# Gates stored as twelve lines, weight measurements two steps later, final scatters of half rows without an order between them, and the eighth block asked for first

## The chip, the cores and the metric

The kernel runs on one core of a Trainium2 chip. The metric is the device time of one execution in microseconds (us). Three runs of the kernel before gave 1245.0, 1250.6 and 1256.08 us, so the median is 1250.6.

## The reference

A block-local attention feeds two mixture-of-experts layers. The attention (2 batches, 8 heads, 768 positions, head size 64) gives `x` with 1536 rows (tokens) of 512. The first layer routes every token to one of 8 experts, the second mixes all 8:

```python
logits = x @ w_gate                      # first layer, N = 1536, E = 8, F = 1024
expert_idx = np.argmax(logits, axis=1)
probs = softmax(logits); gate_w = probs[np.arange(N), expert_idx]
for e in range(E):
    out[mask_e] = gate_w[mask_e, None] * (np.maximum(x[mask_e] @ w1[e], 0) @ w2[e])

P = np.exp(x @ w_gate - max)             # second layer
for _ in range(8):
    P /= P.sum(1, keepdims=True) + 1e-09
    P /= P.sum(0, keepdims=True) + 1e-09
    P *= N / E
for e in range(E):
    out += P[:, e:e+1] * (np.maximum(x @ w1[e], 0) @ w2[e])
```

## The kernel before

The engines are TensorE (PE), VectorE (DVE), ScalarE (ACT), GpSimd (POOL) and SyncE (SP, which only starts DMAs here). Each runs its own instructions in order. Up to the end of the first layer a scheduler of the language sets the order in which each engine gets them; the second layer is written out by hand on a clock of ticks.

**Routing.** While the attention ends, `rows_out` transposes each tile of 128 tokens, copies it out of PSUM on ACT (line 533, three buffers `xn`) and stores it to `xd` in HBM (line 534, SP's queue). `experts`, `ranks` and `by_lane` work out on DVE which expert each token has and which row of which block it takes. `row_i` (line 653) holds the result, and `seat_i` (line 672) the rows to which results go. After the last routing matmul, `warm` (line 174) issues 100 small matmuls on PE, whose results nothing reads.

**First layer.** Tokens are sorted into blocks of 256 rows with one expert each. There are at least `NMIN` = 6 and at most 13; with these inputs there are seven. For each block POOL gathers two tiles of 128 rows (line 1034, `xb<-xd,row_i`; it waits for all stores to `xd`), PE transposes them (1066), ACT and DVE split them into a high part (`xh`, 1071) and a low part (`xl`, 1072), and `layer1` (979) and `layer2` (1001) multiply by weights that are split in the same way (`wh` on ACT at 944, `wl` on DVE at 946). The weights go through a ring of four 512 KB buffers `kx`. The gather of the first block is followed on POOL by a memset of `wgq` (1043).

While block n is computed, `compute` calls `step()` 18 times; the even calls take the next step of loading and splitting weights (`ahead`), the odd ones one list of `more`. `more` holds the gate work and eight pieces of second-layer weights, each as a row of steps (`plain`), a new piece every four steps:

```python
return [lambda: p.load(raw), idle, idle, lambda: p.measure(junk), p.measured, p.rate, ...]
each = -(-len(more) // (NMIN - 1))
```

`measure` (740, ACT) sums the squares of a piece and needs its load to have landed. `gate_square` (1138, ACT) sums the squares of the second gate's weights into `wgq`. `gates` (1155 to 1162: seven operations on DVE, one on ACT) works out each token's gate weight, and `gates_out` (1165) stores it to `gd` with one DMA from a tile of 128 partitions by 12 columns, so that neighbours in a column lie 4 bytes apart in HBM. As far as their operands allow, the scheduler puts these steps earlier than they are written. `gd` is read much later, by the gathers at line 850.

After the sixth block all engines load the number of blocks (1180) and branch:

```python
with tc.If(count > NMIN) as beyond:      # 1208
    rest(NMIN, cur)                      # starts with tc.If(count > n + 1), 1201
with beyond.Else():
    ...                                  # exactly six blocks
```

`rest` fetches and computes further blocks, and its own `Else` runs the last block (`final`). With seven blocks an engine falls through the first branch and jumps at the second.

**Second layer.** `first` (1365) and `second` (1451) compute each expert's products in seven block products of half-size matrices. The tail of the last expert adds the results into `acc` on DVE (1482) and scatters finished rows to `out` from POOL (1486). For the last pair of tiles the products come in the order i = 0, 1, 3, 2, 5, 4, 6: i = 5 completes the upper half of the second tile's rows, i = 4 the first tile, i = 6 the lower half of the second tile. Scatters are at i = 4 and i = 6, whole rows each. All write to the tensor `out`, so each waits for the one before.

## Time and profile before

| what | us |
|---|---|
| median of three runs | 1250.6 |
| the profiled execution | 1249.01 |
| its span, first to last instruction | 1247.2 |
| PE busy in the span | 1181.1 |
| DVE busy | 972.6 |
| ACT busy | 846.0 |
| POOL busy | 265.9 |

All times in the text are microseconds from the start of the span. A row of a timeline gives the start, the duration, the engine, the line, the operation with its operands, how many of them were merged, and in square brackets how long the engine had been idle before it and what it waited for. A wait with several causes is put down to the last one. `PEclk` is the clock that TensorE was granted, as a share of full speed.

### The profile page before, as it was taken

Reading aid. Unit: us, or ns where it says so; the run is one execution under the profiler, and the core shown is the slowest. Engines: PE = TensorE matmul, PEld = TensorE weight load, DVE = VectorE, ACT = ScalarE, POOL = GpSimd, SP = SyncE. Lnnn points to the kernel's source line nnn. Section 1 sums busy time; section 2 is a strip of 40 time slices with the busy share of each in tenths; the row PEclk is TensorE's granted clock in tenths of the full one; section 3 lists DMA queues with packets and bytes.
Section 4 is the critical chain, followed back from the end, with each engine's and each line's share of the span. In section 5 each row is a group of like instructions: output and inputs, shape, how many; then the busy total and the mean of one; then the engine's idle time right before and its main releaser. Section 6 shows DMA issues by size and latency. Waiting matters only on the chain. (4 is left out here: it accounts for less than half of the span.)

```text
span 1247.2 us, 27484 instructions
## 1 busy us (share of the span) xinstructions
PE 1181.1 (95%) x10473; PEld 1044.1 (84%) x10473; DVE 972.6 (78%) x1950; ACT 846.0 (68%) x1595; POOL 265.9 (21%) x331
## 2 busy tenths in 40 slices
PE   6898799999889999999999999999999999999997
PEld 5776688888778788888888888888888888888886
DVE  6695578884588898897878788788978878796763
ACT  5585467774677767776877677677767767776440
POOL 4351212312221220120121112111211211121011
PEclk9899799999999999999999999999999999999999
DMA  9947687862335543665556566555656655663201
GB/s 206 205 97 206 155 275 257 253 208 96 112 111 157 140 130 96 161 148 142 131 119 141 145 162 146 144 115 122 156 137 161 138 135 126 138 149 94 68 35 52
DMA packets 186496, 179.79 MB, mean 144 GB/s; under 512 B 35872, under 2 KB 159520, under 8 KB 185968
## 3 DMA queue, kind: packets, MB, share of 16 engines
q1 hardware_dynamic: 159648, 136.41, 38.6%
q0 software_dynamic: 26704, 41.50, 17.9%
q8 instruction: 85, 1.39, 0.5%
q14 instruction: 59, 0.48, 0.1%
HBM read 131.38 MB, written 15.53 MB: 118 GB/s over the span
## 5 line engine op out<-in xcount | busy, mean ns | idle before, releaser
L1365 PEld LDWEIGHTS <-w1h 128*128 128x128 f16 x2688 | 258.3, 98 | 46.0 <-issue 15.9
L1451 PEld LDWEIGHTS <-hh 128*128 128x128 f16 x2688 | 263.4, 98 | 32.0 <-issue 1.2
L1365 PE MATMUL fx<-kx,w1h 128*128 128x256 f16 x1472 | 257.3, 272 | 8.2 <-ACT c L1372 4.6
L1451 PE MATMUL gx<-w2l,hh 128*128 128x256 f16 x768 | 209.3, 273 | 1.1 <-DVE w2l L780 1.1
L1451 PE MATMUL gx<-w2h,hh 128*128 128x256 f16 x768 | 209.3, 273 | 1.0 <-DVE acc L1482 1.0
L1451 PE MATMUL gx<-w2h,hl 128*128 128x256 f16 x768 | 209.3, 273 | 0.0
L1365 PE MATMUL fx<-kx,w1l 128*128 128x256 f16 x736 | 200.5, 272 | 0.0
L1365 PE MATMUL fa<-kx,w1h 128*128 128x256 f16 x1104 | 193.7, 273 | 0.7 <-ACT yb L1113 0.7
L1372 ACT ACTIVATE c<-fx,kap 128x256 f32<-128x256 f32 x288 | 134.5, 473 | 79.3 <-PE fx L1365 78.8
L1451 PE MATMUL ga<-w2h,hh 128*128 128x256 f16 x576 | 157.6, 274 | 0.0
L1451 PE MATMUL ga<-w2l,hh 128*128 128x256 f16 x576 | 157.6, 274 | 0.0
L1451 PE MATMUL ga<-w2h,hl 128*128 128x256 f16 x576 | 157.5, 273 | 0.0
L1365 PE MATMUL fa<-kx,w1l 128*128 128x256 f16 x552 | 150.7, 273 | 0.0
L1365 PEld LDWEIGHTS <-w1l 128*128 128x128 f16 x1344 | 131.4, 98 | 17.2 <-issue 1.8
L1451 PEld LDWEIGHTS <-hl 128*128 128x128 f16 x1344 | 131.7, 98 | 16.7 <-issue 1.3
L1420 DVE TENSOR_TENSOR hl<-c,hh 128x1024 f16<-128x1024 f32 x96 | 117.1, 1220 | 26.4 <-ACT hh L1417 25.7
L1417 ACT CAST hh<-c 128x1024 f16<-128x1024 f32 x96 | 99.8, 1040 | 34.6 <-DVE c L1414 34.2
L1493 ACT ACTIVATE y<-gx,pws 128x256 f32<-128x256 f32 x144 | 68.2, 474 | 79.9 <-PE gx L1451 62.2
L753 POOL DMA_DIRECT2D raw<-raw x77 | 77.1, 1031 | 210.3 <-DVE w2l L780 97.4
L1375 DVE SCALAR_TENSOR_TENSOR c<-fa,kap,c 128x512 f32<-128x512 f32 x96 | 71.7, 747 | 46.3 <-PE fa L1365 39.9
L1408 DVE SCALAR_TENSOR_TENSOR hl<-c,hh 128x768 f16<-128x768 f32 x96 | 91.2, 950 | 15.4 <-ACT hh L1405 15.4
L1484 POOL DMA_DIRECT2D acc<-y x36 | 31.4, 871 | 336.8 <-ACT c L1372 265.9
(263 smaller groups left out, 2438.6 us busy)
## 6 DMA issues: line engine op xcount, KB each, us to landing
raw<-in_moe_w SPq DMA_DIRECT2D x228, 128.0 KB, 3.5
kx<-in_moe_w SPq DMA_DIRECT2D x56, 512.0 KB, 5.0
kx<-xohd SPq DMA_DIRECT2D x147, 128.0 KB, 3.3
kx<-xold SPq DMA_DIRECT2D x147, 128.0 KB, 3.1
acc<-y POOLq DMA_DIRECT2D x72, 256.0 KB, 4.5
raw<-raw POOLq DMA_DIRECT2D x77, 128.0 KB, 3.6
raw<-in_moe_w SPq DMA_DIRECT2D x38, 256.0 KB, 3.6
vt<-in_v SPq DMA_DIRECT2D x16, 240.0 KB, 7.5
```

The source lines that it names most:

```text
L753: nc.gpsimd.dma_start(out=self.raw[:, to], in_=self.raw[:, of], accum_op=ALU.add)
L1365: nc.tensor.matmul(p, l[:, a, kc * P : (kc + 1) * P], r[:, j, kc], start=new and kc == 0 and m == 0, stop=kc == K2 - 1 and m == 2, skip_gr ...
L1372: nc.scalar.activation(c[:, q], p, f, scale=k_)
L1375: nc.vector.scalar_tensor_tensor(out=c[:, q], in0=x, scalar=k_, in1=c[:, q], op0=ALU.mult, op1=ALU.add)
L1408: nc.vector.scalar_tensor_tensor(out=h[1][:, :3], in0=raw, scalar=0.0, in1=h[0][:, :3], op0=ALU.max, op1=ALU.subtract)
L1417: nc.scalar.copy(h[0][:, 3:], c)
L1420: nc.vector.tensor_tensor(out=h[1][:, 3:], in0=c, in1=h[0][:, 3:], op=ALU.subtract)
L1451: nc.tensor.matmul(p, l, r, start=new and f == 0 and m == 0, stop=f == F2 - 1 and m == 2, skip_group_check=True)
L1484: nc.gpsimd.dma_start(out=to, in_=gs[0], accum_op=ALU.add)
L1493: nc.scalar.activation(gs[h][:, d], p, AF.Copy, scale=w)
```

## The change

1. `gate_square` may not be issued before the latest `layer1` result on ACT; `gates` not before the latest on DVE. `gates` begins at step 3 of `more` in place of 2.
2. `gates_out` first transposes the 128 by 12 gates on PE, copies them to `gt` (12 partitions of 128) on ACT, and stores 12 lines of 512 bytes.
3. In `plain` two more idle steps stand between a piece's load and its measurement; all that follows moves by two. `more` grows from 39 to 41 lists, `each` from 8 to 9 a block.
4. The branch after the sixth block asks first for an eighth block (`rare`), then for a seventh, which is now straight code. PE gets a hint that the first branch is taken.
5. At the end the second tile of each pair is scattered in two halves of 256 columns, at i = 5 and i = 6, through `half_i` (two small DVE operations at tick 118). All final scatters are declared independent of each other.

```diff
         def gate_square():
             sq = wq.tile([P, KC * E], F32, name="wgsq")
-            nc.scalar.activation(sq, wg2_sb, AF.Square, accum_out=wgq)
+            with tc.issue_after(taken[-1][0].ins):
+                nc.scalar.activation(sq, wg2_sb, AF.Square, accum_out=wgq)
...
-            return [lambda: p.load(raw), idle, idle, lambda: p.measure(junk), p.measured, p.rate, lambda: (p.raw_hi(), p.sums(fast=True)), lambda: (p.raw_lo(), p.sum4(fast=True)),
+            return [lambda: p.load(raw), idle, idle, idle, idle, lambda: p.measure(junk), p.measured, p.rate, lambda: (p.raw_hi(), p.sums(fast=True)), lambda: (p.raw_lo(), p.sum4(fast=True)),
...
         def gates():
             sh = [P, NTB, E]
-            nc.vector.tensor_tensor(out=gex, in0=lg, in1=mx.unsqueeze(2).to_broadcast(sh), op=ALU.subtract)
+            with tc.issue_after(taken[-1][1].ins):
+                nc.vector.tensor_tensor(out=gex, in0=lg, in1=mx.unsqueeze(2).to_broadcast(sh), op=ALU.subtract)
...
         def gates_out():
-            nc.sync.dma_start(out=gd.rearrange("(t p) o -> p (t o)", p=P), in_=gate)
+            pt = ps_m.tile([NTB, P], F32, tag="m", name="pt")
+            nc.tensor.transpose(pt, gate, ident)
+            nc.scalar.copy(gt, pt)
+            nc.sync.dma_start(out=gd.rearrange("(t p) o -> t (p o)", p=P), in_=gt)
...
-            [(0, [gate_square, gate_rate]), (2, [gates, lambda: None, gates_out])]
+            [(0, [gate_square, gate_rate]), (3, [gates, lambda: None, gates_out])]
...
+        def hint():
+            tc.mark_branch_hint_location("rare", hint="LikelyTaken", engines=[mybir.EngineType.PE])
...
+                if n == NMIN - 1:
+                    own_ += [[]] * (HINT + 1 - len(own_))
+                    own_[HINT] = own_[HINT] + [hint]
...
-        with tc.If(count > NMIN) as beyond:
-            rest(NMIN, cur)
+        with tc.If(count > NMIN + 1, label="rare") as beyond:
+            nxt, steps = fetch(NMIN + 1)
+            compute(NMIN, cur, steps, nxt)
+            rest(NMIN + 1, nxt)
         with beyond.Else():
-            for fs in early():
-                for f in fs:
-                    f()
+            with tc.If(count > NMIN) as odd:
+                final(NMIN, cur)
+            with odd.Else():
+                for fs in early():
+                    for f in fs:
+                        f()
...
-            if e == E - 1 and i in (4, 6):
-                nc.gpsimd.indirect_dma_start(
-                    out=out, out_offset=bass.IndirectOffsetOnAxis(ap=token_i[:, t : t + 1], axis=0), in_=acc[:, t], in_offset=None,
-                    bounds_check=NT - 1, oob_is_err=True,
+            if e == E - 1 and i in (4, 5, 6):
+                if i == 4:
+                    to, at_, rows, n = out, token_i[:, t : t + 1], acc[:, t], NT
+                else:
+                    to, at_ = out.rearrange("t (h d) -> (t h) d", h=2), half_i[:, t - HTB, 6 - i : 7 - i]
+                    rows, n = acc[:, t, d], 2 * NT
+                put = nc.gpsimd.indirect_dma_start(
+                    out=to, out_offset=bass.IndirectOffsetOnAxis(ap=at_, axis=0), in_=rows, in_offset=None,
+                    bounds_check=n - 1, oob_is_err=True,
                 )
+                tc.declare_no_dep(put.ins, group="rows", reason="disjoint rows")
+                tc.add_to_no_dep_group("rows", put.ins)
```

How the change moves instructions, at three places. The line numbers in the rows of the change are its own, two to thirty above those of before.

**Routing, SP and ACT.** SP's queue at the end of the attention, before: the last loads of weights for the second layer (`raw`), the stores of rows (`xd<-xn`), the store of the gates (`gd<-gate`), then loads of block numbers.

```order
L167 DMA raw_93<-in_moe_w 128x256
L534 DMA xd<-xn 128x512 x3
L1165 DMA gd<-gate 128x12x1
L534 DMA xd<-xn 128x512 x3
L1045 TENSOR_LOAD eblk_i
L1045 ISA x2
```

The same place in the change:

```order
L169 DMA raw_94<-in_moe_w 128x256
L167 DMA raw_95<-in_moe_w 128x2x256
L168 DMA raw_95<-in_moe_w 128x256
L169 DMA raw_95<-in_moe_w 128x256
L536 DMA xd<-xn 128x512 x6
L1047 TENSOR_LOAD eblk_i
L1047 ISA x2
L1128 TENSOR_LOAD eblk_i
```

The store of the gates no longer stands among the stores of rows; it comes late in the second block, between loads of first-layer weights (`L1172 DMA gd<-gt 12x128`). ACT at the same place, before: copies of rows, the exponential of the gates (`gex`), measurements of three pieces (`raw,ssq`), the gate's squares (`wgsq,wgq`), the branch for the first expert (`eblk_i`), then the first weight split:

```order
L533 COPY xn<-pr 128x512 x2
L1156 ACTIVATE gex<-gex 128x96
L533 COPY xn<-pr 128x512 x4
L740 ACTIVATE raw_91,ssq_1730<-raw_91 128x1024
L1138 ACTIVATE wgsq,wgq<-wg_sb 128x32
L740 ACTIVATE raw_92,ssq_1730<-raw_92 128x1024
L740 ACTIVATE raw_93,ssq_1730<-raw_93 128x1024
L1126 TENSOR_LOAD eblk_i
L1127 COMPARE_AND_BRANCH
L1127 UNCONDITIONAL_BRANCH x2
L944 CAST wh_1763<-kx 128x1024
```

In the change:

```order
L535 COPY xn<-pr 128x512 x6
L742 ACTIVATE raw_93,ssq_1732<-raw_93 128x1024
L742 ACTIVATE raw_94,ssq_1732<-raw_94 128x1024
L742 ACTIVATE raw_95,ssq_1732<-raw_95 128x1024
L1128 TENSOR_LOAD eblk_i
L1129 COMPARE_AND_BRANCH
L1129 UNCONDITIONAL_BRANCH x2
L946 CAST wh_1765<-kx 128x1024
```

The exponential and the squares are gone from this place; the squares stand behind the first block's `layer1`, the exponential inside the second block.

**The branch, PE.** Before, after the sixth block's last product (`py`): the load of the block count, two branches, and the seventh block's first products (`ph`):

```order
L1001 MATMUL py_3499<-wh_1767,hl 128x512
L1180 TENSOR_LOAD nblk_i
L1208 COMPARE_AND_BRANCH
L1201 COMPARE_AND_BRANCH
L979 MATMUL ph<-xh_1786,wh_1769 128x256
```

In the change one branch stands here, and what follows it in the listing is the eighth block's code; the seventh block's stands behind that of all rarer counts, after a second branch (`L1229 COMPARE_AND_BRANCH`):

```order
L1003 MATMUL py_3506<-wh_1769,hl 128x512
L1196 TENSOR_LOAD nblk_i
L1224 COMPARE_AND_BRANCH
L981 MATMUL ph<-xh_1788,wh_1771 128x256
L981 MATMUL ph<-xl_1789,wh_1771 128x256
```

The hint was written into the sixth block, but the scheduler put it at the start of PE's program, ahead of the attention's first transposes:

```order
L1651 UNCONDITIONAL_BRANCH
L1651 BRANCH_PREFETCH_HINT
L297 MATMUL pt_142<-ident,kt 128x96 x4
L297 MATMUL pt_143<-ident,kt 128x96 x4
L297 MATMUL qt<-ident,qt 128x96 x8
```

The branch that it names is the one that stands at 290.7 us in the trace of before.

**The end, POOL.** Before, the last additions into `acc` by DMA, twelve scatters, the end of the program:

```order
L1484 DMA acc<-y 128x512
L1495 DMA acc<-y 128x512
L1486 DMA out<-acc,token_i 1536x512 x12
L1619 UNCONDITIONAL_BRANCH
L1619 ISA
```

In the change there are eighteen; the last of them, with the same end:

```order
L1516 DMA out<-acc,token_i 1536x512
L1516 DMA out<-acc,half_i 3072x256 x2
L1516 DMA out<-acc,token_i 1536x512
L1516 DMA out<-acc,half_i 3072x256
L1651 UNCONDITIONAL_BRANCH
L1651 ISA
```

The last scatter now moves 256 columns of 128 rows in place of 512, and its other half is issued two scatters earlier.

## Rows read from the trace of the kernel before

**Rows 1.** The page: span, and TensorE's granted clock in 40 slices.
```profile
span 1247.2 us, 27484 instructions
...
PEclk9899799999999999999999999999999999999999
```

**Rows 2.** Windows of stages: length, busy time (instructions) by engine, clock, DMA share, GB/s.
```profile
118.00:142.30 24.30, 13.93 (x163) 12.02 (x161) 12.27 (x58) 9.49 (x19) 5.61 (x8) 0.81 0.73 110
...
190.00:215.00 25.00, 25.00 (x162) 22.54 (x161) 21.72 (x40) 19.48 (x31) 6.75 (x6) 1.00 0.80 263
```

**Rows 3.** SP's queue around the store of the gates, timeline.
```profile
118.84 1.78 SPq L534 DMA_DIRECT2D xd<-xn  x3
121.05 0.37 SPq L1165 DMA_DIRECT2D gd<-gate  x1
121.85 4.20 SPq L534 DMA_DIRECT2D xd<-xn  x3
```

**Rows 4.** Windows of 1 us before and after that store, columns as in rows 2.
```profile
120.00:121.00 1.00, 1.00 (x19) 0.90 (x18) 1.00 (x9) 0.28 (x1) 0.00 (x0) 1.00 0.90 332
...
126.00:127.00 1.00, 1.00 (x13) 1.00 (x11) 0.86 (x5) 0.00 (x0) 0.00 (x0) 0.50 0.90 33
```

**Rows 5.** POOL, the gather of the first block's two tiles, timeline.
```profile
134.82 1.17 POOL L1034 DMA_INDIRECT xb<-xd,row_i  x1 [8.89 <-DMA xd<-xn]
136.30 1.05 POOL L1034 DMA_INDIRECT xb<-xd,row_i  x1 [0.30 <-issue]
```

**Rows 6.** DMA issues: count, KB each, median us to landing.
```profile
kx<-in_moe_w SPq DMA_DIRECT2D x56, 512.0 KB, 5.0
...
xd<-xn SPq DMA_DIRECT2D x12, 256.0 KB, 2.6
```

**Rows 7.** ACT, routing, timeline.
```profile
125.12 0.59 ACT L533 COPY xn<-pr 128x512 f32<-128x512 f32 x1 [2.75 <-DMA xd<-xn]
127.33 1.06 ACT L740 ACTIVATE raw<-raw 128x1024 bf16<-128x1024 f32 x1 [1.63 <-DVE seat_i L672]
...
137.50 0.23 ACT L1138 ACTIVATE wgsq<-wg_sb 128x32 f32<-128x32 f32 x1 [9.02 <-POOL wgq L1043]
...
139.81 1.98 ACT L944 CAST wh<-kx 128x1024 fp32r<-128x1024 f32 x2
```

**Rows 8.** PE, from the warming matmuls to the first block, timeline.
```profile
125.31 7.55 PE L174 MATMUL warm<-ones_b 128*128 128x128 bf16 x100
138.52 0.45 PE L1066 MATMUL pt<-ident,xb 128*128 128x128 f32 x1 [5.66 <-DMA xb<-xd,row_i]
...
144.58 0.58 PE L979 MATMUL ph<-xl,wh 128*128 128x256 f32 x1 [1.25 <-DVE xl L1072]
...
145.17 0.41 PE L979 MATMUL ph<-xh,wh 128*128 128x256 f32 x1
145.38 0.41 PE L979 MATMUL ph<-xl,wh 128*128 128x256 f32 x1
```

**Rows 9.** DVE, weight and row splits ahead of that product, timeline.
```profile
141.56 2.37 DVE L946 TENSOR_TENSOR wl<-kx,wh 128x1024 fp32r<-128x1024 f32 x2
143.84 1.28 DVE L1072 TENSOR_TENSOR xl<-pt,xh 128x512 fp32r<-128x512 f32 x2
```

**Rows 10.** The latest measurement that waited, ACT, timeline.
```profile
249.80 1.06 ACT L740 ACTIVATE raw<-raw 128x1024 bf16<-128x1024 f32 x1 [2.77 <-DMA raw<-in_moe_w]
```

**Rows 11.** PE, the wait behind that measurement, timeline.
```profile
252.33 0.39 PE L979 MATMUL ph<-xh,wh 128*128 128x256 f32 x1 [1.54 <-DVE hl L985]
```

**Rows 12.** PE, behind the branch to the seventh block, timeline.
```profile
297.58 0.28 PE L979 MATMUL ph<-xl,wh 128*128 128x256 f32 x1 [2.61 <-issue]
297.70 0.28 PE L979 MATMUL ph<-xh,wl 128*128 128x256 f32 x1
```

**Rows 13.** PE's queue, line 1201: duration in ns (min/median/max), first and last start.
```profile
L1201 PEldq COMPARE_BRANCH  x2: 182/1775/3368, 290.7 to 317.3; - x2
```

**Rows 14.** DVE, the last sum into the result, timeline.
```profile
1238.17 0.48 DVE L1482 SCALAR_TENSOR_TENSOR acc<-gx,pws,acc 128x256 f32<-128x256 f32 x1 [0.56 <-PE gx L1451]
```

**Rows 15.** POOL, the last two scatters, timeline.
```profile
1237.89 0.98 POOL L1486 DMA_INDIRECT out<-acc,token_i  x1 [4.68 <-DVE acc L1482]
1241.36 0.98 POOL L1486 DMA_INDIRECT out<-acc,token_i  x1 [2.49 <-DMA out<-acc,token_i]
```

More of the change, by code (lines that the diff above doesn't have):

```diff
@@ L137, in body @@
     gse = const.tile([P, NTB], F32, name="gse")
+    gt = const.tile([NTB, P], F32, name="gt")
+    half_i = const.tile([P, HTB, 2], U32, name="half_i")
     nblk_i = const.tile([1, 1], I32, name="nblk_i")
@@ L1177, in body @@
             else:
-                compute(n, cur, steps, nxt, more[each * (n - 1) : each * n])
+                own_ = [list(x) for x in more[each * (n - 1) : each * n]]
+                if n == NMIN - 1:
+                    own_ += [[]] * (HINT + 1 - len(own_))
+                    own_[HINT] = own_[HINT] + [hint]
+                compute(n, cur, steps, nxt, own_)
             cur = nxt
@@ L1276, in start1, with halves @@
             nc.vector.tensor_reduce(out=st[0], in_=lg2, axis=AX.XY, op=ALU.max)
+        def halves():
+            for h in range(2):
+                nc.vector.tensor_scalar(half_i[:, :, h], token_i[:, HTB:], 2, h, op0=ALU.mult, op1=ALU.add)
         def start2():
@@ L1313, in end @@
             weigh(0)
-        return [start1, start2, start3] + [turn1, turn2, turn3] * 8 + [end]
+        return [start1, start2, start3] + [turn1, turn2, turn3] * 8 + [end, halves]
     def weigh(e):
@@ L1511, in body @@
     turns = [66 + 6 * i + t for i in range(8) for t in (0, 2, 4)]
-    for tick, f in zip([55, 58, 62] + turns + [115], mix):
+    for tick, f in zip([55, 58, 62] + turns + [115, 118], mix):
         at(tick, f)
```

3 lines of the change are left out of this document (2 added, 1 removed).

## The prediction

> **What bounds the kernel now.** The page first: TensorE (PE) is near its full clock except in a few slices near the start [rows 1]. So I looked for places where PE waits, and read the windows of each stage next. Inside the first layer PE is covered (25.00 of 25 us busy from 190 to 215), but between 118 and 142.3 us it works 13.93 of 24.30 us, at a mean clock of 0.81 [rows 2]. That is the routing stage, where the change moves most. There I read SP's queue, then POOL, ACT and PE in order of time.
>
> SP starts three stores of rows by 120.62, then the store of the gates, then three more stores [rows 3]. Before it the DMA engines moved 332 GB/s at a busy share of 0.90; five microseconds later they are as busy (0.90) and move 33 GB/s [rows 4]. Something with very small pieces fills them, and the gates' 1536 single numbers are the only such transfer here. The stores of rows sit behind it: the first gather waits for them until 134.82 [rows 5], though the median store lands 2.6 us after its issue [rows 6]. Even ACT's last copy of rows, at 125.12, had to wait 2.75 us for a store [rows 7].
>
> The gather holds more than PE. `gate_square` needs the memset that POOL issues behind the gather, so ACT stands still for 9.02 us with two measurements and the first weight split behind it [rows 7]. PE ends its warming matmuls at 132.86, idles 5.66 us, transposes at 138.52 [rows 8], and the first product that needs `xl` runs at 144.58. By then its clock has halved: products start 0.21 us apart [rows 8], at full clock 0.12 us [rows 12].
>
> **The change part by part.** All sums are made against the profiled execution, 1249.0 us: its span of 1247.2 and 1.8 us around it that no part of the change touches. It lies 1.6 us under the median of the runs.
>
> *Routing.* With the store of the gates gone, I give the row stores their median. The third, issued at about 120.3, lands near 122.9; the sixth copy follows (0.59 us), its store lands 2.6 us later, near 126.1 [rows 3, 6, 7]. The gather can start there, 8.7 us earlier; its rows came 3.7 and 4.9 us after its start [rows 5, 8], so near 131. PE is then the later one: its warming ends at 132.86, or some 0.3 us sooner, because seven gate operations leave the DVE chain ahead of it, where most were hidden by waits. PE transposes in about 1 us (from 132.6 to 133.6). ACT no longer stops: three measurements of 1.06 us each from about 127.0 end near 130.3, the first split ends by 131.3 and the second by 132.3 (1.98 us for two), then comes `xh`. DVE does its part of the sums, two splits `wl` in 2.37 us up to about 134.1, and the first half of `xl` (1.28 us for two, so 0.7) [rows 9]. The product that began at 144.58 begins near 134.8: 9.8 us gained. Until 149.9 before, some 24 products ran at half clock; at 0.12 in place of 0.21 us each they save 2.2 us, if the clock holds through the short gap. Together 12.0.
>
> I take 11.0. The weights for `layer2` are loaded into buffers that the `wl` splits free, near 133; they land 5.0 us later in the median [rows 6], and PE now wants the first of them near 138. That leaves nothing to spare, so about 1 us may be waited for. The bounds are 6 (the clock's 2.2 us and 3.8 more, most of one landing, lost to weights that come late) and 12.
>
> *The gates' new place.* Eight small DVE and ACT operations, one transpose and one copy go into the second block. Their sum is about 1.5 us on DVE; PE is busy 25.00 of 25 us just behind there [rows 2], and nothing reads `gd` before the last block. Cost 0; if DVE were the later engine at that place, up to 1.5.
>
> *Later measurements.* ACT waited 2.77 us for a load at 249.80, and PE 1.54 us behind it [rows 10, 11]. Two steps are four of 18 calls of a block of some 25 us, about 5.6 us, more than ACT waited. This wait goes. What could be late next is DVE: nine lists a block in place of eight pack the same pieces denser into blocks two to four, and DVE is busy 21.72 of 25 already [rows 2]. Even if all of it grew by an eighth it would be 24.4 of 25, which still fits. I take 1.5 gained, bounds 0 and 1.9.
>
> *The branch.* PE stands 2.61 us behind the branch, with no engine to wait for [rows 12]; the jump itself took 3.37 us in PE's queue, most of it beside running matmuls [rows 13]. A hint that works could take the 2.61 us; one that was forgotten on the way takes nothing, and the code's new place could shift the stall either way by about as much. The hint stands at the very start of PE's program, and no row tells how long it holds. Bounds 2.6 lost and 2.6 gained; with an even chance of a working hint I take the middle of nothing and all, 1.3.
>
> The Trainium skill (Runtime: NRT & Kernel Launch, section "Instruction fetch mechanics") speaks against this part: prefetch is purely sequential, and a taken branch out of the window forces a fetch of the target page before the engine goes on. It knows no hint. The long jump of rows 13 agrees with the second half; by this rule the branch term is 0 and the forecast 1.3 us higher.
>
> *The end.* The last sum ends at 1238.65 [rows 14]. The last scatter could go then, but started at 1241.36, because it waited 2.49 us for the scatter of 1237.89 to land [rows 15]. In the change, the first half of the second tile goes before that one, at about 1236.3. The scatter of 1237.89 keeps its time, occupies POOL until 1238.87, and 0.3 us later (the step between two gathers in rows 5) the last half follows, at 1239.2: 2.15 us gained. It cannot be before 1238.9 (2.5), and as two scatters are now in flight together it could land up to 1 us later (1.2). Six scatters more on POOL, about 1 us each, fall into waits of 4.68 us and the like. The two operations on `half_i` cost DVE 0.3 us at a place where nobody waits for it.
>
> **Sum.** 11.0 + 1.5 + 1.3 + 2.15 = 15.95, so 1249.0 becomes 1233.0; for a median that stands where that of before stood, 1.6 more: about 1234.
>
> **Rivals.**
>
> *Weights become the wait.* If the first block's weights arrive late, the gain of routing falls to its lower bound of 6, because a block that starts sooner only stands sooner before an empty ring. For it: the 5.0 us to landing against a need after 5. Against it: loads are issued when splits end, and these move as far forward as PE. Without the hint's gain: 6 + 1.5 + 2.15 = 9.65, so about 1241.
>
> *The hint does nothing and the clock falls again.* The clock already stood at 0.50 from 126 to 127 us, behind the routing's small matmuls [rows 4]. PE's gap after warming is now split by transposes, but if the clock falls, 2.2 us go, and the branch gives 0: 11.0 - 2.2 + 1.5 + 2.15 = 12.45, so about 1238.
>
> *Slower: the hint keeps the fetch from what comes next.* It is armed at the first instruction and names a target that is 290 us away. If it takes, all the way, a place that the next piece of code would need, PE stands at each crossing as it does behind the branch. At 2.6 us a crossing [rows 12] this outweighs the other gains (14.65 without the branch) from six crossings on; with ten it is 26 us, so about 1262. Against it: in before PE shows such a stall only at the branch, so I have nothing that says code fetch has no room.
>
> *Not what it says.* The scatters could still be ordered by the queue itself: then the end gains at most the shorter last transfer, and the time is 1236.
>
> **How the numbers follow.** The forecast as worked out, with the gain of the hint anywhere between nothing and all: 0.66, from 1229 to 1238. The clock falling and no hint: 0.12, at 1238. Late weights: 0.14, at 1241. Ordered scatters: 0.04, at 1236. The slow rival: 0.04, at 1262. The range of 8 in 10 goes from 1228 (routing 12, measurements 1.9, branch 2.6, end 2.5 make 19.0, and two more for runs that lie lower) to 1242, which takes in the late weights. A change of 1%, 12.5 us or below 1238.1, is about what a measurement of this kernel can tell from none. Faster by more than that: 0.72 (nearly all of the forecast, ordered scatters, half of the second rival); within 1%: 0.24; slower by more: 0.04.
>
> **What would show it.** Right, if in the profile of the change the first gather on POOL starts near 126, ACT has no wait for `wgq`, the `xl` product stands near 135 with the clock at 1.00, no measurement on ACT waits for its load in the middle blocks, and the last scatter starts about half a microsecond after the last sum of DVE. The branch term is read directly: PE's wait before the seventh block. The forecast is wrong if the gather starts at 126 and the second block begins less than 8 us earlier than now (then weights are the wait), if PE's slices behind 126 still show 0.50 into the first block, or if waits without a cause are spread over PE's first 290 us.

## The result, and the profile after

The changed kernel takes 1233.46 us (median of four runs, 1231.43 to 1235.67) against 1249.46 us before: 0.987 of it, with an interval of 0.982 to 0.992. The forecast was 1234. The time was right; of the four terms from which it came one was close, for another reason than the one given, and three were off by about 2 us, in both directions. That the misses cancel is luck.

The page of the changed kernel (answers to [rows 1]) shows the shorter span, and a clock that still dips in the fifth slice; where the time went has to be read from places.

```profile
span 1232.5 us, 27503 instructions
...
PEclk8999899999999999999999999999999999999999
```

A warning for the whole comparison: the two profiled runs differ by 1.7 us before the change begins. The first warming matmul starts at 123.61, before at 125.31 [rows 8], though up to there PE's instructions are the same; in the runs below it starts anywhere from 122.06 to 126.18, and 1.66 of the 1.70 us are there already at PE's 251st matmul, a third of the way through the attention. So all times are counted from that matmul. "On before's clock" below means 1.70 us added.

The routing stage, by windows of the same length as in [rows 2] (length, busy time and instructions by engine, clock, DMA share, GB/s): PE works 19.69 of 24.30 us instead of 13.93. But in the window of 25 us further on, full before, it now lacks 2.16 us. The windows cover the same time, not the same work: by then the changed kernel is some 9 us further on.

```profile
116.30:140.60 24.30, 19.69 (x207) 18.14 (x206) 18.13 (x60) 13.63 (x22) 9.00 (x8) 0.86 0.60 201
188.30:213.30 25.00, 22.84 (x149) 20.41 (x148) 20.47 (x36) 18.71 (x30) 6.17 (x6) 1.00 0.78 252
```

POOL's timeline, the first block's gather and the last two scatters (answers to [rows 5, 15]): the gather waits 2.06 us for stores instead of 8.89, and nothing orders the last scatters.

```profile
126.30 1.18 POOL L1036 DMA_INDIRECT xb<-xd,row_i  x1 [2.06 <-DMA xd<-xn]
127.78 1.25 POOL L1036 DMA_INDIRECT xb<-xd,row_i  x1 [0.30 <-issue]
...
1227.19 0.98 POOL L1516 DMA_INDIRECT out<-acc,token_i  x1 [0.59 <-DVE acc L1507]
1228.48 0.99 POOL L1516 DMA_INDIRECT out<-acc,half_i  x1 [0.30 <-issue]
```

ACT's timeline (answers to [rows 7]). The wait for `wgq` is gone. Two things that the sum had too small or not at all stand here: the last copy still waits 2.08 us for a store, and the first split waits 1.30 us for SP. The last row is a measurement in the third block.

```profile
122.83 0.59 ACT L535 COPY xn<-pr 128x512 f32<-128x512 f32 x1 [2.08 <-DMA xd<-xn]
...
130.16 1.99 ACT L946 CAST wh<-kx 128x1024 fp32r<-128x1024 f32 x2 [1.30 <-SPq L1129]
...
201.21 1.06 ACT L742 ACTIVATE raw<-raw 128x1024 bf16<-128x1024 f32 x1 [3.55 <-DMA raw<-in_moe_w]
```

PE's timeline (answers to [rows 8, 11, 12]): the first `xl` product comes 10.65 us behind the first warming matmul, before 19.27. The wait of 2.16 us is new, 0.97 us of the wait of [rows 11] are left, and in place of the 2.61 us behind the branch PE waits 1.00 us, some 30 products later, for DVE.

```profile
123.61 7.37 PE L176 MATMUL warm<-ones_b 128*128 128x128 bf16 x100
...
134.26 0.40 PE L981 MATMUL ph<-xl,wh 128*128 128x256 f32 x1 [0.94 <-DVE xl L1074]
...
207.95 0.66 PE L1068 MATMUL pt<-ident,xb 128*128 128x128 f32 x4 [2.16 <-DVE gsc L683]
...
243.21 0.39 PE L981 MATMUL ph<-xh,wh 128*128 128x256 f32 x1 [0.97 <-DVE hl L987]
...
289.89 0.39 PE L981 MATMUL ph<-xh,wh 128*128 128x256 f32 x1 [1.00 <-DVE hl L987]
```

The branch's first compare in the engines' queues (line 1224; ns min/median/max, first start; answers to [rows 13]), then the second (line 1229), which ACT and DVE reach only 2.5 and 2.9 us behind the first, PE after 0.5:

```profile
L1224 PEldq COMPARE_BRANCH  x1: 373/373/373, 280.8 to 280.8; - x1
L1224 DVEq COMPARE_BRANCH  x1: 63/63/63, 286.2 to 286.2; - x1
L1224 ACTq COMPARE_BRANCH  x1: 45/45/45, 286.3 to 286.3; - x1
```

```profile
L1229 ACTq COMPARE_BRANCH  x2: 38/39/40, 288.8 to 311.3; - x2
L1229 DVEq COMPARE_BRANCH  x2: 47/48/50, 289.0 to 311.0; - x2
```

The end. DVE's last sum starts at 1227.48 (answers to [rows 14]) and the span ends 5.03 us later, before 9.02. Only 2.19 us of these 3.99 lie in the start of the last scatter (1.00 us behind the start of that sum, before 3.19). The rest lies in POOL's closing drain, of the changed kernel first, then of the kernel before (ns; it is the longest of three):

```profile
1227.48 0.48 DVE L1507 SCALAR_TENSOR_TENSOR acc<-gx,pws,acc 128x256 f32<-128x256 f32 x1 [0.56 <-PE gx L1476]
```

```profile
L1651 POOLq DRAIN  x3: 46/113/3462, 1228.0 to 1232.2; - x3
```

```profile
L1619 POOLq DRAIN  x3: 46/113/5214, 1241.1 to 1246.9; - x3
```

It starts at 1228.01 and lasts until 1231.47, 2.99 us behind the start of the last scatter; before it ended at 1246.35, 4.99 us behind it.

The ledger of the two profiled runs, each entry the change of the way between two marks:

| stretch | gained, us | forecast |
|---|---|---|
| attention (same instructions, chance) | 1.70 | 0 |
| first warming matmul to first `xl` product | 8.62 | 9.8 |
| on to the ninth `xh`·`wh` product of block 3 | -0.09 | 2.2 of clock, less 1 for weights |
| on to that product of block 6 | -0.54 | 1.5 |
| on to the 13th of block 7 (the branch) | 1.83 | 1.3 |
| on to the last sum | -0.83 | 0 |
| last sum to the end | 3.99 | 2.15 |
| sum | 14.68 | 15.95 |

### The profile page after: what moved, and what is told of

It reads as the page before. It is cut to its first block, busy times and chain, and to the rows that moved or that the text cites. A ratio compares the mean times of both kernels' runs of the same rounds, so it can differ in the third digit from the quotient of the medians.

```text
span 1232.5 us, 27503 instructions
## 1 busy us (share of the span) xinstructions
PE 1178.5 (96%) x10474; PEld 1041.9 (85%) x10474; DVE 972.9 (79%) x1952; ACT 847.3 (69%) x1596; POOL 273.7 (22%) x337
## 4 chain that ended last, share of the span: by engine, by line
PE 62%; issue 11%; DMA 6%; DVE 6%; ACT 3%; POOL 1%; POOLq 0%; SPq 0%; ACTq 0%; DVEq 0%
PE fx L1390 16%; PE gx L1476 16%; PE fa L1390 12%; PE ga L1476 12%; PE ph L981 4%; DMA yd<-yb,seat_i 3%; PE py L1003 3%; POOL out L1516 1%; DMA kx<-xold 1%; DVE wl L948 1%; DMA kx<-in_moe_w 1%; ACT wh L946 1%; DMA acc<-y 1%; DMA raw<-in_moe_w 1%; ACT raw L742 0%
## 6 DMA issues: line engine op xcount, KB each, us to landing
raw<-in_moe_w SPq DMA_DIRECT2D x228, 128.0 KB, 3.5
kx<-xohd SPq DMA_DIRECT2D x147, 128.0 KB, 3.1
kx<-xold SPq DMA_DIRECT2D x147, 128.0 KB, 3.2
raw<-raw POOLq DMA_DIRECT2D x77, 128.0 KB, 3.7
```

## The experiments

All runs in one table. "Start" is the first warming matmul; the next four columns count from it: to the first `xl` product, to the ninth `xh`·`wh` product of blocks 3 and 6, and to the thirteenth of block 7. "End" is from the start of DVE's last sum. All columns but the median are of one profiled execution. Times of single runs in the first layer scatter by 1 to 3 us even with the same code, so a cause is read from its own rows. The kernel before, measured again beside the runs, has medians from 1249.77 to 1250.34 us.

| run | median | start | `xl` | block 3 | block 6 | block 7 | end |
|---|---|---|---|---|---|---|---|
| before | 1249.46 | 125.31 | 19.27 | 74.42 | 148.36 | 176.10 | 9.02 |
| changed | 1233.46 | 123.61 | 10.65 | 65.89 | 140.37 | 166.28 | 5.03 |
| thin_early | 1239.35 | 124.41 | 16.27 | 70.75 | 144.90 | 171.11 | 5.02 |
| square_early | 1234.61 | 124.24 | 12.60 | 67.07 | 140.48 | 166.33 | 5.03 |
| hint_act | 1232.40 | 122.06 | 10.57 | 65.25 | 138.55 | 164.31 | 5.00 |
| hint3 | 1231.42 | 124.33 | 10.63 | 66.85 | 140.25 | 165.05 | 5.01 |
| half_ordered | 1238.19 | 122.57 | 10.61 | 64.41 | 137.01 | 162.86 | 11.43 |
| whole_free | 1237.00 | 124.87 | 10.60 | 65.55 | 139.45 | 165.66 | 6.89 |
| measure_old | 1233.55 | 124.78 | 10.63 | 65.23 | 139.04 | 165.19 | 5.01 |
| best1 | 1230.61 | 122.19 | 12.30 | 67.27 | 140.98 | 165.75 | 5.02 |
| before_shift | 1245.99 | 123.73 | 19.49 | 74.58 | 148.95 | 175.02 | 9.02 |
| thin_late | 1239.02 | 126.18 | 10.63 | 65.47 | 144.69 | 170.81 | 5.02 |
| best2 | 1233.97 | 125.64 | 10.66 | 65.41 | 140.83 | 165.62 | 5.02 |
| best3 | 1226.83 | 125.93 | 8.55 | 60.57 | 134.63 | 159.39 | 5.02 |

**thin_early: the store of single numbers, back at its old place.**

```diff
-            with tc.issue_after(taken[-1][1].ins):
-                nc.vector.tensor_tensor(out=gex, in0=lg, ...
+            nc.vector.tensor_tensor(out=gex, in0=lg, ...
 ...
-            nc.tensor.transpose(pt, gate, ident)
-            nc.scalar.copy(gt, pt)
-            nc.sync.dma_start(out=gd.rearrange("(t p) o -> t (p o)", p=P), in_=gt)
+            nc.sync.dma_start(out=gd.rearrange("(t p) o -> p (t o)", p=P), in_=gate)
```

> The changed kernel, but the gates are worked out and stored where they were before: 1536 single numbers, between the third and the fourth store of rows; gate_square stays at its new place. My theory (the store alone holds the gather): with attention as in the changed kernel's profile the first gather starts near 133 instead of 126.3, the stores of rows around it land after 5 us or more instead of 2.0, the first xl product comes near 140 (not 143, since ACT is no longer held behind gate_square), and the time is 5 to 6.5 us above the changed kernel, 1238.5 to 1240. Rival A (ACT's stand behind gate_square was what counted): xl product near 135 to 136, time within 1.5 us of the changed kernel. Rival B (both are needed for the gain, either one alone gives back all): xl product near 143, time 8 to 9 us above, near 1242.

Measured: 1239.35 us, 5.9 above the changed kernel. POOL's timeline: the gather starts 8.80 us behind the first warming matmul instead of 2.69, and the `xl` product comes at 16.27 instead of 10.65.

```profile
133.21 1.30 POOL L1036 DMA_INDIRECT xb<-xd,row_i  x1 [8.17 <-DMA xd<-xn]
```

So 5.62 of the 8.62 us come from the store, as my theory had it, and the other 3.0 need `gate_square` moved as well. The eight gate operations went back with the store, but the waits name the stores of rows: the gather's 8.17 us, and 8.20 us in front of ACT's last copy. Rivals A and B fall.

**square_early: `gate_square` among the measurements again.**

```diff
-            with tc.issue_after(taken[-1][0].ins):
-                nc.scalar.activation(sq, wg2_sb, AF.Square, accum_out=wgq)
+            nc.scalar.activation(sq, wg2_sb, AF.Square, accum_out=wgq)
```

> The changed kernel, but gate_square has no place given and goes second among ACT's measurements, as before. My theory: ACT stops from 126.7 until POOL's memset behind the two gathers (129.1 in the changed kernel's profile), 2.4 us instead of 9.0, of which 1.3 us are hidden because the first split waits for SP anyway; the first xl product is 1 to 2 us later than 134.3, time 1 to 2 us above the changed kernel. Rival A (ACT has slack for all of it): xl product within 0.3 us of 134.3, no difference. Rival B (the stop is as long as before): 6 us or more.

Measured: ACT waits 2.38 us for the memset, and the `xl` product is 1.95 us later; the total is 1.15 us above the changed kernel, within their scatter. At block 6 the 1.95 us are no longer seen (140.48 against 140.37), but five runs with the changed kernel's code up to there lie from 137.01 to 140.37, so how much of a small gain of routing reaches the end stays open.

```profile
129.78 0.23 ACT L1141 ACTIVATE wgsq<-wg_sb 128x32 f32<-128x32 f32 x1 [2.38 <-POOL wgq L1045]
```

**hint_act: the hint for ACT in place of PE; the rest of the code keeps its place.**

```diff
-            tc.mark_branch_hint_location("rare", hint="LikelyTaken", engines=[mybir.EngineType.PE])
+            tc.mark_branch_hint_location("rare", hint="LikelyTaken", engines=[mybir.EngineType.Activation])
```

> The changed kernel with the same code at the same places, but the hint is given to ACT instead of PE. My theory (the hint itself moves the target's code in ahead of time): PE stands 2 to 3.4 us at the branch before the seventh block again, ACT's gap between its two compares there (2.46 us in the changed kernel) falls under 0.3 us, DVE's gap stays near 2.9; the time is 1 to 2 us above the changed kernel, not 2.6, because PE's 1.0 us wait for the first hl goes. Rival (the code's new place took the stall away, not the hint): PE has no stall without it either, time within 0.5 us.

Measured: 1232.40 us, no slower than the changed kernel. PE's jump takes 3.41 us again, ACT's way between its compares is 0.50 us instead of 2.50, DVE's stays at 2.89. But PE has no wait at the branch: its queue was far enough ahead, and the jump lies beside running matmuls. The rival was right: the hint works, but PE did not need it. Its wait for `hl` some 30 products later, which I had expected to go, is still 0.68 us, with DVE late alone.

```profile
L1224 PEldq COMPARE_BRANCH  x1: 3408/3408/3408, 277.4 to 277.4; - x1
L1224 DVEq COMPARE_BRANCH  x1: 63/63/63, 282.8 to 282.8; - x1
L1224 ACTq COMPARE_BRANCH  x1: 74/74/74, 282.9 to 282.9; - x1
```

```profile
L1229 ACTq COMPARE_BRANCH  x2: 43/47/51, 283.4 to 307.8; - x2
L1229 DVEq COMPARE_BRANCH  x2: 47/48/50, 285.7 to 307.5; - x2
```

```profile
286.37 0.39 PE L981 MATMUL ph<-xh,wh 128*128 128x256 f32 x1 [0.68 <-DVE hl L987]
```

**hint3: the hint for PE, ACT and DVE.** The edit is the list of engines, as above, with all three.

> The changed kernel with the hint given to PE, ACT and DVE. My theory: each engine fetches its own code, so ACT's gap (2.46 us between its compares) and DVE's (2.87 us) go as PE's did, PE no longer waits 1.0 us for hl behind the branch, and the time is about 1 us under the changed kernel. Rival A (the engines share one place for a hinted target, or one fetch path): at least one of the three keeps a gap of 2 us or more. Rival B: the gaps go, but PE's wait stays because DVE and ACT are late there for another reason; time as the changed kernel.

Measured: all three jumps are short (PE 0.46; ACT and DVE reach line 1229 0.5 and 0.6 us behind line 1224, at 286.9 and 286.8). PE's wait for `hl` is gone, and block 6 to block 7 takes 24.80 us instead of 25.91. That holds in every profile: the four runs with three hints (hint3, best1, best2, best3) take 24.76 to 24.80 us for this stretch, the other runs with the changed code there 25.76 to 26.21. The median lies 2.0 us under the changed kernel, about 1.1 of it from here; no row shows the rest.

```profile
L1229 ACTq COMPARE_BRANCH  x2: 43/47/51, 287.4 to 310.7; - x2
L1229 DVEq COMPARE_BRANCH  x2: 54/62/69, 287.5 to 310.4; - x2
```

**half_ordered and whole_free: the two halves of the end, one at a time.**

```diff
 half_ordered
-                tc.declare_no_dep(put.ins, group="rows", reason="disjoint rows")
-                tc.add_to_no_dep_group("rows", put.ins)
 whole_free
-            if e == E - 1 and i in (4, 5, 6):
-                if i == 4:
+            if e == E - 1 and i in (4, 6):
+                if True:
```

> The changed kernel, but each of the last scatters waits for the one before it to land, as before (half rows kept). My theory: without leave to overlap, the half rows lose what they gained and more, since three landings follow each other: the scatter of the whole tile starts about 0.3 us after the first half lands, the last half 0.3 us after the whole tile lands, so the last scatter starts near 3.7 us behind the last sum of DVE instead of 1.0, 2.7 us later. As to the closing drain of POOL (it ended 4.99 us after the start of the last scatter before, 2.99 us in the changed kernel): if its length follows the size of the last scatter (A), it stays near 3.0 us here; if it follows the scatters' waiting for each other (B), it is near 5 us again. Total 2.7 us above the changed kernel by A, 4.5 us by B.

> The changed kernel, but the last tile goes out as one scatter of whole rows; the scatters may overlap. My theory: the last scatter starts as in the changed kernel, about 1.0 us behind the last sum, so the leave to overlap alone makes the start 2.2 us earlier than before and the half rows add nothing to that. The closing drain: by (A, size of the last scatter) it ends near 5.0 us after the last scatter starts, 2 us more than in the changed kernel; by (B, the scatters' waiting for each other) near 3.0 to 3.4. Total 2 us above the changed kernel by A, within 0.4 us by B.

Measured: the end takes 11.43 us with ordered halves and 6.89 us with free whole rows (changed 5.03, before 9.02). Ordered, the last two scatters wait 2.21 and 2.55 us for the one before, so the last one starts 7.4 us behind the last sum; I had said 3.7, because I had let only these two wait. The scatters before them wait as well, and the first of the three starts 0.69 us behind that sum; in the changed kernel it starts 1.86 us ahead of it. Without an order it starts 1.01 us behind that sum with whole rows too. The drain ends 2.98 us behind the last scatter's start with half rows in order, 2.99 without one, and 5.03 us with whole rows: (A). POOL's timelines and drains, half_ordered then whole_free:

```profile
1223.24 0.98 POOL L1516 DMA_INDIRECT out<-acc,half_i  x1 [2.22 <-DVE acc L1507]
1226.44 0.98 POOL L1516 DMA_INDIRECT out<-acc,token_i  x1 [2.21 <-DMA out<-acc,half_i]
1229.97 0.98 POOL L1516 DMA_INDIRECT out<-acc,half_i  x1 [2.55 <-DMA out<-acc,token_i]
```

```profile
L1649 POOLq DRAIN  x3: 46/113/3202, 1229.7 to 1233.7; - x3
```

```profile
1229.54 0.99 POOL L1516 DMA_INDIRECT out<-acc,token_i  x1 [0.30 <-issue]
```

```profile
L1651 POOLq DRAIN  x3: 46/113/5513, 1229.1 to 1235.1; - x3
```

So of 3.99 us, 2.13 come from dropping the order (9.02 to 6.89) and 1.86 from the half rows (6.89 to 5.03), all of it through the drain.

**measure_old: the measurements two steps earlier again.**

```diff
-            return [lambda: p.load(raw), idle, idle, idle, idle, lambda: p.measure(junk), ...
+            return [lambda: p.load(raw), idle, idle, lambda: p.measure(junk), ...
-            + [(4 * (2 * F2 - 1) + 8, [level])]
+            + [(4 * (2 * F2 - 1) + 6, [level])]
```

> The changed kernel with the measurements of the second layer's weights two steps earlier, as before. My theory: the wait of PE for a PSUM buffer in front of the transposes at 207.95 (2.16 us in the changed kernel, 0.7 to 1.4 in three other runs) goes, because no pf stands directly in front of transposes on PE; PE's wait behind the measurement that waits for its load (1.54 us before, 0.97 in the changed kernel) comes back to about 1.5; PE's way from the first xl product to the fourth block's 169th xh product, 129.7 us in the changed kernel, shortens by about 1 us: moving the measurements was no gain. Rival A (the move is worth what I forecast): it lengthens by 1.5 us. Rival B (another wait fills the place): unchanged within 0.4 us.

Measured: 1233.55 us, as the changed kernel. The wait at the transposes goes, but PE waits 1.33 and 1.57 us at 169.9 and 194.7 instead. Block 3 to block 6 takes 73.81 us; five runs with the new place and the same code there (changed, hint_act, hint3, half_ordered, whole_free) take 72.60 to 74.48, and before 73.94. The longer stretch that the expectation names, from the first `xl` product to block 6, is 1.3 us shorter (128.4 for 129.7), but those five runs take 126.4 to 129.7. Rival B: neither a gain nor a loss that can be told. ACT's waits from 140 to 310 us (total in us, number, longest) agree, in the order before, changed, measure_old: the measurements wait 3.7 and 4.9 us for their loads at the old place, and 3.6 to 6.4 in those five runs at the new one.

```profile
ACT raw L740 <- DMA raw<-in_moe_w: 3.7, 2, 2.8
```

```profile
ACT raw L742 <- DMA raw<-in_moe_w: 5.2, 2, 3.6
```

```profile
ACT raw L742 <- DMA raw<-in_moe_w: 4.9, 3, 2.5
```

**before_shift: the kernel before with eight more warming matmuls.**

```diff
-        warm(ps_s, "s", 100, last.ins)
+        warm(ps_s, "s", 108, last.ins)
```

> The kernel before with 8 more warming matmuls (16 more instructions on PE ahead of the branch; PE stands idle 5.66 us behind them anyway). Open is what took away PE's stand of 2.61 us four products behind the jump. Theory A (where the code lies: the jump brings in one piece of code and the next piece begins four products after the target, so PE waits for a second fetch): with 16 instructions more in front, the place where PE stands moves by 16 instructions, eight products earlier, so ahead of the target; then only the jump's own fetch is left, beside running matmuls, and PE stands less than 0.5 us there. Total 2 to 3 us under before. Theory B (the stand follows the jump in time, wherever the code lies): PE stands 2 to 3 us again, three to six products behind the jump; total as before.

Measured: 1245.99 us, 0.9967 of before (interval 0.9954 to 0.9981; ten runs, and fifteen of before beside them with a median of 1250.34). Work that nobody needs makes the kernel 4 us faster in the median; its profile shows 1.67 of them at the branch (block 6 to block 7: 26.07 us instead of 27.74). The jump takes 3.31 us as ever, the 2.61 us are gone, and PE waits 0.99 us for `hl` some 30 products later, just as in the changed kernel. Theory A, as far as one profile of each kernel tells. The traces' packets of code fit it: of those of 16 KB (queue q8) one lies near 291.7 in before, at PE's jump, and the next near 295.3, inside the stand that ends at 297.58; in before_shift that next one lies near 293.9, beside running products. The trace does not name the engine that they are for. The rest of the 4 us is not explained by a row.

```profile
L1201 PEldq COMPARE_BRANCH  x2: 182/1745/3308, 289.7 to 314.7; - x2
```

```profile
298.75 0.38 PE L979 MATMUL ph<-xh,wh 128*128 128x256 f32 x1 [0.99 <-DVE hl L985]
```

**thin_late: single numbers at the new place.** The edit is the second half of that of thin_early.

> The changed kernel with the gates worked out at their new place in the second block, but stored as 1536 single numbers (no transpose, no copy). My theory: the store fills the DMA engines for some 8 to 14 us wherever it goes, as it did before at 120.6 to 134; here weight loads lie beside it, and PE waits 2 to 6 us for late splits in the second or third block; total 2 to 6 us above the changed kernel. Rival (the ring of four buffers has that much slack): no wait over 0.5 us more than in the changed kernel, no difference; then the twelve lines were not needed, only the new place.

Measured: 1239.02 us, 5.6 above the changed kernel; PE waits 3.89 us at 202.36, and block 3 to block 6 takes 79.2 us instead of 74.5. The store starts at 180.7; the windows before it and behind it (columns as above) show the DMA engines as busy as ever, with 51 GB/s instead of 328. So the new place alone would have given back about as much as taking the store out of routing gained (5.62 us): the twelve lines are needed.

```profile
176.00:180.00 4.00, 4.00 (x25) 3.57 (x25) 3.97 (x11) 2.14 (x6) 0.34 (x1) 1.00 0.98 328
...
188.00:192.00 4.00, 4.00 (x32) 3.70 (x31) 3.31 (x9) 3.64 (x7) 1.33 (x1) 1.00 1.08 51
```

```profile
202.36 0.58 PE L981 MATMUL ph<-xh,wh 128*128 128x256 f32 x1 [3.89 <-DVE wsc L686]
```

**best2: the rate of the third piece one call later, and the hint for three engines.**

```diff
-p.measured, p.rate, ...                                idle, p.sum_hi, p.sum_lo]
+p.measured, *([idle] if i == 2 else []), p.rate, ...   *([] if i == 2 else [idle]), p.sum_hi, p.sum_lo]
```

> The changed kernel with two edits: the hint given to PE, ACT and DVE, and the third piece's rate one call later, so that its pf stands behind the transposes on PE. My theory: no wait of PE at the transposes near 208 (0.3 to 2.2 us in the runs so far), none for hl behind the branch (0.7 to 1.3 us): 1 to 3 us under the changed kernel, 1230.5 to 1232.5. Rival (as with the older place of the measurements, another wait of that size takes the place): 1 us under it at most, from the branch alone.

Measured: 1233.97 us. The wait at the transposes is gone, and PE waits 0.53 and 1.90 us a little later, for ACT's `hh` and DVE's `hl` (PE's timeline). ACT is late there: its measurement had waited 2.48 us for a load, and from then on it has no idle time up to that place (ACT's timeline). The rival was right, and the branch's microsecond stands in the rows (24.79 us from block 6 to block 7) but doesn't show in the median.

```profile
219.53 0.38 PE L981 MATMUL ph<-xh,wh 128*128 128x256 f32 x1 [1.90 <-DVE hl L987]
```

```profile
212.01 1.06 ACT L742 ACTIVATE raw<-raw 128x1024 bf16<-128x1024 f32 x1 [2.48 <-DMA raw<-in_moe_w]
```

**best1 and best3: a shorter way through routing.** best1 lets SP read the later blocks' experts behind the first weight loads, puts the first three measurements behind the first splits, and has both edits of best2. best3 has six buffers `xn` and 70 warming matmuls on top.

```diff
 best1
+                with tc.issue_after(sent[3].ins) if 0 < n <= NMIN else ExitStack():
                     got["e"] = nc.sync.value_load(eblk_i[0:1, n : n + 1], min_val=0, max_val=E - 1)
+                with tc.issue_after(cuts[PIN[i]][0].ins) if i < 3 else ExitStack():
                     p.measure(junk)
 best3, further
-            xn = a3.tile([P, DM], F32, tag="xn", name="xn")
+            xn = a3.tile([P, DM], F32, tag="xn", name="xn", bufs=6)
-        warm(ps_s, "s", 100, last.ins)
+        warm(ps_s, "s", 70, last.ins)
```

Here `sent[3]` is the fourth load of weights for the first block's `layer2`, `cuts` are its first splits, and `PIN` is (1, 3, 3).

> The changed kernel with four edits: SP reads the later blocks' experts behind the first weight loads, so that its first branch comes near 126.5 instead of 129.77; the first three measurements go behind the first splits on ACT; the third piece's rate goes one call later, so that its pf stands behind the transposes and not in front of them; the hint is given to PE, ACT and DVE. My theory: ACT's first split starts near 127.5 instead of 130.16, the first xl product 0.7 to 1.5 us earlier counted from the first warming matmul (10.65 us in the changed kernel), bound by the second gather's rows, which land at 131.33; the wait of 0.7 to 2.2 us before the transposes near 208 goes; PE waits for no hl behind the branch. Together 2 to 4 us under the changed kernel, 1229.5 to 1231.5. Rival A: the measurements, now in the first block, delay splits there, and PE waits as much in the first block as was gained; gain 1 to 2 us. Rival B: loads into the ring become the wait, first product earlier but second block not; gain 1 to 2 us.

> The four edits of the run best1, and two more: six buffers for the rows on their way to HBM instead of three, so that ACT's last copy doesn't wait 2.08 us for a store and the first gather can start some 2 us earlier, ahead of the weight loads that held it in best1 (its second gather landed 5.5 us after its start instead of 3.6); and 70 warming matmuls instead of 100, so that PE is free when the rows land. My theory: counted from the first warming matmul, the gather starts near 0.7 us instead of 2.7, both gathers have landed by 6 us, and the first xl product comes near 8 us instead of 10.65; total 2 to 4 us under best1, 1227 to 1229. Rival A: the loads still hold the second gather, product near 10 to 12 us, total as best1. Rival B: fewer warming matmuls let the clock fall for longer in the first block, which takes back 2 us.

Measured for best1: 1230.61 us, but not by routing. The first split came 3.09 us behind the first warming matmul instead of 6.55, its buffers were free early, and the weight loads went out early (127.6 and 128.7). Beside them the second gather took 1.92 us on POOL and landed 5.5 us after its start instead of 3.6. The `xl` product came at 12.30, later than in the changed kernel: a form of rival B. Of the 2.9 us in the median 1.1 lie at the branch; no row shows the rest.

```profile
126.59 1.92 POOL L1040 DMA_INDIRECT xb<-xd,row_i  x1 [0.30 <-ACT wh L947]
```

Measured for best3: 1226.83 us (1224.23 to 1230.02), 0.981 of before (0.9785 to 0.9837), the fastest of all; every run lies under every run of the changed kernel. ACT's copies no longer wait, the gathers start 1.74 and 3.21 us behind the first warming matmul, ahead of the loads, and the product comes at 8.55. The clock stays at 1.00 in the first block, so rival B fell. By block 3 it leads the changed kernel by 5.3 us, more than the 2.1 us of routing. The other 3.2 us lie where the clock falls in the changed kernel's profile: its windows from the first `xl` product to the second block, and on to the ninth `xh`·`wh` product of block 3, stand first, those of best3 behind them. With the clock at 1.00 PE is busy 1.61 and 1.37 us less for the same products. What keeps the clock up in best3 is not shown.

```profile
127.67 1.17 POOL L1040 DMA_INDIRECT xb<-xd,row_i  x1 [16.52 <-DVE seat L673]
129.14 1.06 POOL L1040 DMA_INDIRECT xb<-xd,row_i  x1 [0.30 <-issue]
```

```profile
134.26:159.24 24.98, 24.71 (x149) 22.40 (x149) 15.10 (x22) 13.02 (x23) 5.80 (x6) 0.93 0.76 250
159.24:189.50 30.26, 28.51 (x180) 25.59 (x180) 23.90 (x46) 22.23 (x37) 7.00 (x7) 0.94 0.80 254
```

```profile
134.48:157.58 23.10, 23.10 (x149) 21.15 (x150) 20.33 (x34) 18.46 (x32) 6.30 (x6) 1.00 0.85 286
157.58:186.50 28.92, 27.14 (x180) 24.24 (x179) 21.21 (x46) 19.84 (x35) 6.51 (x7) 1.00 0.82 262
```

## Why the time was right and three of its terms were not

**Routing: mechanism right, 11.0 us too much, 8.5 measured.** The store of single numbers did hold the gather, and `gate_square` the rest (thin_early, square_early). The first `xl` product gained 8.62 us instead of 9.8. Two steps of the working failed. "The third, issued at about 120.3, lands near 122.9" took the median landing of 2.6 us; it landed 4.16 us after its issue (118.57 to 122.73), so the last copy waited 2.08 us and the gather started at 128.0 on before's clock instead of 126.1. And "the first split ends by 131.3" forgot SP: the split waits until SP has left its first branch, and six reads of the later blocks' experts and one of the number of blocks stand ahead of that in SP's queue, from 125.8 to 129.8. In this run the second step set the product: the rows were transposed by 132.35 and the first half of `xh` was done at 132.64, but DVE was at the two weight splits until 133.5.

The 2.2 us of clock did not last. In the changed kernel's own profile they are hardly there: the products stay at half clock until 137.9, the sign that the prediction had named for being wrong, and from the first `xl` product to the seventh `xh`·`wl` takes 3.75 us, before 4.01. In hint_act, hint3, half_ordered and whole_free, with the same code there, it takes 2.25. But in all five the clock falls again near the start of the second block, to 0.50 for 3.4 us (6.8 in hint3) from 160 or 162 us on, behind waits of PE for `xh` and `xl` of 1.3 to 1.9 us (0.94 in the changed kernel's second window under best3); in before it stands at 1.00 there. So at block 3 these five runs lead before by 7.6 to 10.0 us, about what routing alone gave. What decides is not shown: before_shift has such a fall too, and thin_early, with such waits, has none. Late weights cost little: PE waits 0.58 and 0.26 us for `wl` in the first block of hint3 and whole_free, before not at all, and the second block begins 9.0 to 10.7 us earlier in the five runs. That rival, which needed less than 8, fell.

**The gates' new place:** nothing speaks against its 0, with the twelve lines, but no run takes it by itself; thin_late shows what it would have cost without them.

**Later measurements: wrong, 1.5 us forecast, none there.** "This wait goes" named the wrong cause. The measurements wait because loads come late, and a later place lets other measurements wait for other loads: 5.2 us in all against 3.7. That late loads are the limit is argued from these waits; no run takes it by itself. The new wait of 2.16 us is made so: the measurement of 201.21 had waited 3.55 us, its `pf` went to PE just in front of the transposes and took one of their two buffers, and DVE freed it at 207.74. I had watched DVE's busy time, not the place of `pf` on PE.

**The branch: 1.3 forecast, 1.83 measured, for another reason.** I gave the gain to the hint, and left the code's new place, which I had named, in the bounds. The 2.61 us depend on where the code lies (before_shift, hint_act); the hint takes some 3 us off PE's jump, which running matmuls hid anyway. And what would be late next was not asked here: ACT and DVE jump without a hint and cost PE 1.00 us. By the Trainium skill (Runtime: NRT & Kernel Launch, section "Instruction fetch mechanics") code comes in blocks, in sequence, and a taken branch out of the window waits for its target. The jump of 3.3 to 3.4 us without a hint agrees, and a second stand that 16 instructions move away is what blocks of code would make. That prefetch is only sequential does not hold with a hint: 0.37 to 0.46 us.

**The end: 2.15 us forecast, 2.19 there, and 1.80 more that no term had.** The last scatter started as worked out. What ends the span is POOL's drain, and I had counted only to the scatter: its change, 4.99 to 2.99 us behind the scatter's start, stood at nothing in the sum.

So 4.5 us too much in routing and measurements met 2.4 us too little at branch and end, and 1.7 us of attention by chance, of which the second layer took back 0.8: there the clock stood at 0.91 from 340 to 360 us, and at 1.00 at the same place before. That the sum holds is luck. In the profiled run the second rival came true (the hint gave PE nothing, and the clock fell in the first block); that the time is not its 1238 comes mostly from the code's place and the drain, 3.6 us that it had at nothing. The other rivals did not occur: no wait without a cause is spread over PE's first 290 us, and no queue orders the scatters.

## What to carry to other kernels

Store small results in long lines: 1536 single numbers cost 5.6 us at either of two places, so moving them away only moves the cost. Before a wait that comes from late loads is shifted by a few steps, add up all waits of that kind: if loads are the limit, a later place need not lower the total. Follow the end of a kernel to the last drain, and the entry of a stage through every queue, the one that only starts DMAs too.

## What the runs showed of the hardware that I had not expected

- POOL's closing drain ends 5.0 us after the start of a last scatter of 128 whole rows (three runs: 4.99, 5.03, and before_shift 4.99) and 3.0 us after one of half rows (2.97 to 2.99 in eleven runs), though the landings differ little (2.7 and 2.4 us).
- A hint set at 0.8 us still shortens the jump at 281 us, for each engine by itself: PE 3.4 to 0.4 us, ACT's way between the compares 2.5 to 0.5, DVE's 2.9 to 0.6.
- Sixteen instructions more in front of a branch took away a stand of 2.61 us behind it, in one profile of each.
- TensorE's clock fell to 0.50 for 3.4 to 6.8 us in the second block in eight of the twelve profiles of the changed kernel and its variants, behind waits of PE of 1 to 3 us there; in thin_early, square_early, measure_old and best3 it stayed at 1.00.
